# Memory read in the projections' PSUM banks, value sums in one run behind the scores, and a later start of the early modulation rows

## The chip, the cores and the metric

One core of a Trainium2 chip runs the whole program. Its engines are called PE (TensorE, matrix products), PEld (PE's weight loads), DVE (VectorE), ACT (ScalarE), POOL (GpSimd) and SP (SyncE, which issues the DMA transfers). Each engine works through its own instructions in program order. The metric is the device time of one execution in microseconds (us); lower is better.

## The reference

The program is one transformer block over 2048 tokens of 1024 channels, in fp32. Cut to what matters:

```
mod = (silu(c) @ w_mod).reshape(1, 6, 1, 1024)      # sa, ca, ga, sb, cb, gb
h = layernorm(x) * (1 + ca) + sa
x = x + ga * A(h)                                   # attention with a memory
h = layernorm(x) * (1 + cb) + sb
x = x + gb * B(h)                                   # MLP across the tokens
# A: 32 heads of 32 channels, 4 segments s of 512 tokens
q, k, v = h @ wq, h @ wk, h @ wv
for s in range(4):
    a_dot = softmax(q_s k_s^T / sqrt(32) + causal mask) @ v_s
    a_mem = phi(q_s) @ M / (phi(q_s) @ z + 1e-6)    # phi(t) = t + 1 if t > 0 else exp(t)
    o_s   = g * a_mem + (1 - g) * a_dot             # g = sigmoid(beta), per head
    M, z  = M + phi(k_s)^T v_s, z + sum(phi(k_s))
A = o @ wo
# B: W2 gelu(W1 layernorm(h)^T + b1) + b2 along the token axis, 3584 hidden rows
```

## The kernel before

**Stages.** The first 110 us load the modulation, normalize the first segment and transpose it. Then comes the attention, until about 950 us: 32 units of work, each one group of four heads (128 channels) in one segment. The first pass (units 0 to 15) takes segments 0 and 1 of the eight groups in turn, the second pass (units 16 to 31) segments 2 and 3. So odd units, and all units from 16 on, have a segment above 0 and read the memory. After the attention come the product with `wo`, the second normalization, and the token MLP (products named `mx`).

**A unit.** `project(t, piece)` has four pieces. Pieces 0 and 1 make keys and values of half the tokens each: 48 products of 256 columns into a PSUM bank `nps`. Piece 2 transposes the keys (bank `kps`), makes the queries (24 products of 512 columns, bank `qps`), splits both into a high and a low part (`sg`; ACT copies, DVE subtracts) and forms `pq` = phi(q) (two ACT steps on `rq`, then DVE) and `pk` = phi(k). Piece 3 splits the values for the sums (`vp`) and calls `memory(t)`. All these banks have the tag `pj`, of which there are two that are used in turn. A bank is used again when the engines that read its last content are done.

**The memory.** `memory(t)` reads the memory in two halves: PE multiplies `pq` by `MZ` into a bank (tile `rd`), DVE adds 1e-6 to the denominators and inverts them (tile `rdd`) and multiplies (tile `am`, line 454). The sum that updates the memory goes to a tile `up`. Before the change, `rd`, `up`, the transposed row maxima (`nmps`) and the transposed outputs (`ops`) all use the tag `ms`, which is one single bank.

**A head.** Steps are counted in heads, n = 4 t + h, 128 in all. Step n calls `scores` for head n, `maxima` for head n + 3, `values` for head n - 2 and a piece of `project` for head n + 8. `maxima` makes the scores once to find each row's maximum (tiles `sx`, `sy`, `sz` in two banks `s1`; DVE reduces each, line 480, which an order names ISA, a second row reading the maximum out). `scores` makes them again transposed (tiles `a0` of 512 columns, `a1` of 384, `a2` of 128 + 256, in two banks `s2`), ACT takes the exponentials into `p32`, POOL cuts the triangle, ACT copies to fp16 (`ph`, the high part) and POOL subtracts for the low part, which lies in the same tile as `p32`. `values` makes the weighted sums on PE: 10 products of 97 columns with the high part and 10 of 65 with the low part, into the one bank `pv`; DVE then inverts, reduces and scales.

**What sets the order.** The code above is not written in issue order. A scheduler places the instructions of each engine by its own estimate of when operands and banks come free, keeping to data and bank dependencies; `tc.issue_after(x)` and `behind(n, engines)` add the rule that what is inside stands after the marked instruction x. `marks[n, "A"]`, `"G"`, `"V"` hold such instructions of head n for ACT, POOL and DVE. Banks of one tag go round in the order in which the code asks for them: `nps` of both halves, `kps`, `qps`, and again `nps`.

**Extra work between heads.** `plan` and `later` put other steps at a head n: splitting the first pass's weights, normalizing the tokens of later segments (`token_tile`), the columns of the modulation (`mod_fetch` loads 128 rows of `w_mod`, `mod_late` reduces them on DVE, line 573), and the scaling of `wo`. All their loads share three buffers with the tag `raw`.

Of the kernel before, what the change touches and what calls it, by code (L numbers as in the profile page):

```python
# [18 lines left out]
P = 128  # L19
# [8 lines left out]
NV = 97  # L28
# [3 lines left out]
VL = 2  # L32
ML0 = 36
# [8 lines left out]
def attention_and_mlp(ctx, tc, x, wq, wkv, wo, beta, w1, b1, w2, b2, c, wm_a, wm_b, out):  # L42
# [19 lines left out]
    a = par.__enter__()  # L62
# [9 lines left out]
    def bank(tag, bufs, name):  # L72
        return psum.tile([P, 512], F32, tag=tag, bufs=bufs, name=name)
# [367 lines left out]
    def memory(t):  # L441
        pr, g, seg = its[t]
        d = st[t]
        d["am"] = am = b.tile([P, 4, 128], F32, tag="am", bufs=3, name=f"am{t}")
        if seg:
            for half in range(2):
                ps = bank("ms", 1, f"rd{t}_{half}")[:, 0:264].rearrange("p (a n) -> p a n", a=2)
                for aa in range(2):
                    i = 2 * half + aa
                    T.matmul(ps[:, aa], d["pq"][:, 128 * i:128 * i + 128], MZ[:, g], start=True, stop=True)  # L450
# [3 lines left out]
                V.tensor_tensor(am[:, 2 * half:2 * half + 2].rearrange("p a (h e) -> p a h e", h=4),  # L454
                                ps[:, :, 0:128].rearrange("p a (h e) -> p a h e", h=4),
                                rd.unsqueeze(3).to_broadcast([P, 2, 4, 32]), op=ALU.mult)
        if seg < 3:
            ps = bank("ms", 1, f"up{t}")
            for i in range(4):
                T.matmul(ps[:, 0:132], d["pk"][:, i], d["v32"][:, i], start=(i == 0), stop=(i == 3))  # L460
# [46 lines left out]
    def scores(t, h):  # L507
# [10 lines left out]
        T.matmul(b1_[:, 0:384], k[:, 128:256], q[:, 128:512], start=True, stop=True)  # L518
        A.activation(p32[:, 512:896], b1_[:, 0:384], AF.Exp, scale=SCALE, bias=shift)
        b2_ = bank("s2", 2, f"a2_{t}_{h}")  # L520
        T.matmul(b2_[:, 0:128], k[:, 384:512], q[:, 384:512], start=True, stop=True)
        T.matmul(b2_[:, 128:384], k[:, 256:384], q[:, 256:512], start=True, stop=True)  # L522
        A.activation(p32[:, 896:1280], b2_[:, 0:384], AF.Exp, scale=SCALE, bias=shift)  # L523
        for base, step in ((0, 512), (896, 128)):
            w = bass.AP(tensor=p32.tensor, offset=p32.offset + base, ap=[p32.ap[0], [step, 2], [1, 128]])
# [6 lines left out]
    def values(t, h):  # L532
# [7 lines left out]
        for part, w in ((0, NV), (1, 65)):  # L540
            for i in range(4):
                for j in range(i + 1):
                    o = col[j](i)
                    T.matmul(pv[:, i, 0:w], ph[part][:, o:o + 128], d["vp"][:, j, h, 0:w], start=(n == 0),  # L544
                             stop=(n == 19), skip_group_check=True)
                    n += 1
        V.reciprocal(pv[:, :, 0], pv[:, :, 0])
        red = r_.tile([P, 4, 32], F32, tag="red", bufs=2, name=f"red{t}_{h}")
        V.tensor_reduce(red, pv[:, :, 1:97].rearrange("p a (c e) -> p a e c", c=3), axis=AX.X, op=ALU.add)
# [108 lines left out]
    def later(n, fetch, m, f, engines):  # L658

        got = []  # L660
        plan(n, lambda: got.append(fetch()))
        plan(m, lambda: f(got[0]), engines)
# [13 lines left out]
                  n + n1, lambda r, g=g, kind=kind, part=part: split_part(g, kind, part, r), "A")  # L676
        plan(n + 4, lambda g=g: keep_w(g))
    for j in range(32):
        n = ML0 + 2 * j + (8 if j >= 8 else 0)
        later(n, lambda j=j: mod_fetch(j), n + (2 if j < 8 else 1), lambda r, j=j: mod_late(j, r), "V")  # L680
    plan(WO0 - 3, lambda: spread(gaw, 0))
    for i in range(8):
        n = WO0 + WOS * i
# [2 lines left out]
    for n in range(-LEADS, 4 * NI + VL):  # L686
        at(scores, n)
        at(maxima, n + LEADS)
        at(values, n - VL)
        m = n + LEADP  # L690
        if 0 <= m + 4 < 4 * NI:
            t = (m + 4) // 4
# [448 lines left out]
```

## Time and profile before

| | |
|---|---|
| median of 3 runs | 2231.71 us (2225.53 to 2231.82) |
| the profiled execution | 2226.6 us |
| its span, first to last instruction | 2224.9 us |
| PE busy | 2190.3 us |
| DVE busy | 1666.7 us |
| ACT busy | 1135.7 us |
| POOL busy | 725.8 us |
| TensorE clock granted, mean | 0.997 |

How to read the rows that follow: a row of a group of instructions has the source line, the engine, the operation, output<-input, the shape and the number of instructions, then after the bar the busy time in us and the mean length of one in ns, then how long the engine was idle before them and who ended that. PE's products overlap: the length of one product includes its way through the array, so the time that a product takes from the next is the distance of starts and not its length. A row of the timeline has the start in us, the length in us, engine, line and operation, and `xN` for N merged instructions. A row of stretches has the stretch, its length, the busy time of each engine with the count of its instructions, and the granted clock (1.00 is full).

### The profile page before, as it was taken

The page shows a single profiled execution, that of the slowest core. Times are in us where ns is not written, and L with a number is a line of the kernel's source. Part 1 is how long each engine was busy: PE and PEld are TensorE (multiplying, and loading weights), DVE is VectorE, ACT ScalarE, POOL GpSimd, SP SyncE. Part 2 cuts the span into 40 slices and gives each one's busy share as a digit, 9 for nine tenths or more (in the row PEclk, how much of TensorE's full clock was granted, in tenths as well). Part 3 has the DMA queues.
Part 4 walks back from the last instruction along what each step waited for, and adds up shares of the span by engine and source line. Part 5 has one row for each costly group of instructions (what it writes and reads, how often), then busy time and mean ns, then how long its engine had stood idle before and what let it go on. Part 6 is the DMA issues. An engine that isn't in the chain of part 4 may idle for free.

```text
span 2224.9 us, 38052 instructions
## 1 busy us (share of the span) xinstructions
PE 2190.3 (98%) x13786; PEld 1881.0 (85%) x13786; DVE 1666.7 (75%) x3762; ACT 1135.7 (51%) x2050; POOL 725.8 (33%) x831
## 2 busy tenths in 40 slices
PE   8999999999999999999999999999999999999999
PEld 5988898888999999888888888888888888888887
DVE  7676777756777777664858766888888886969687
ACT  5486776756666666654636533533334242424232
POOL 2175766646767776663002200033330000000000
PEclk9999999999999999999999999999999999999999
DMA  7666666686556666664754687655556542414134
GB/s 287 192 187 191 175 181 193 189 279 216 170 180 205 188 183 211 193 219 143 231 194 186 226 304 275 243 223 220 204 202 219 206 148 64 145 57 147 57 123 151
DMA packets 175183, 423.03 MB, mean 190 GB/s; under 512 B 17524, under 2 KB 71828, under 8 KB 166036
## 3 DMA queue, kind: packets, MB, share of 16 engines
q1 hardware_dynamic: 174996, 420.61, 57.5%
q8 instruction: 109, 1.79, 0.3%
q14 instruction: 78, 0.64, 0.1%
HBM read 244.62 MB, written 125.06 MB: 166 GB/s over the span
## 4 chain that ended last, share of the span: by engine, by line
PE 87%; DVE 5%; DMA 3%; ACT 2%; POOL 1%; issue 1%; SPq 0%; DVEq 0%; ACTq 0%
PE mx L921 48%; PE nps L192 11%; PE po L791 8%; PE qps L200 7%; PE pv L544 3%; PE a L515 1%; PE sz L478 1%; PE sx L478 1%; DMA sk<-nt 1%; PE up L460 1%; PE a L518 1%; POOL p L530 1%; PE a L522 1%; PE sy L478 1%; PE rd L450 1%
## 5 line engine op out<-in xcount | busy, mean ns | idle before, releaser
L921 PE MATMUL mx<-bU,sp 128*128 128x512 f32 x2352 | 534.3, 389 | 0.9 <-DVE ac L928 0.9
L921 PEld LDWEIGHTS mx<-bU,sp 128*128 128x128 f32 x2352 | 441.3, 188 | 93.4 <-issue 1.3
L119 ACT CAST sp<-wr 128x384 fp32r<-128x384 f32 (+2 forms) x408 | 218.1, 547 | 431.8 <-PE mx L921 349.1
L192 PE MATMUL nps<-wv,h 128*128 128x256 f32 x3072 | 431.2, 283 | 1.6 <-DVE h L122 0.7
L921 PE MATMUL mx<-bA,sp 128*128 128x512 f32 x1764 | 430.5, 389 | 0.0
L530 POOL TENSOR_TENSOR p<-p,ph 128x640 f16<-128x640 f32 x256 | 380.2, 1485 | 138.5 <-ACT ph L528 134.5
L192 PEld LDWEIGHTS nps<-wv,h 128*128 128x128 f32 x3072 | 400.3, 189 | 9.4 <-DVE h L122 2.0
L921 PEld LDWEIGHTS mx<-bA,sp 128*128 128x128 f32 x1764 | 331.2, 188 | 68.7
L122 DVE TENSOR_TENSOR sp<-wr,sp 128x384 fp32r<-128x384 f32 (+2 forms) x408 | 259.8, 648 | 24.7 <-ACT sp L119 24.4
L928 DVE TENSOR_TENSOR ac<-mx,ac 128x512 f32<-128x512 f32 x280 | 189.9, 687 | 85.2 <-PE mx L921 84.1
L200 PE MATMUL qps<-h,wq 128*128 128x512 f32 x768 | 197.9, 400 | 0.0
L528 ACT CAST ph<-p 128x1280 f16<-128x1280 f32 x128 | 161.4, 1261 | 59.7 <-POOL p L526 59.6
L791 PE MATMUL po<-wo,ots 128*128 128x512 f32 x768 | 180.9, 391 | 0.0
L791 PEld LDWEIGHTS po<-wo,ots 128*128 128x128 f32 x768 | 142.7, 188 | 28.7
L200 PEld LDWEIGHTS qps<-h,wq 128*128 128x128 f32 x768 | 141.6, 190 | 27.7
L921 PE MATMUL mx<-bB,sp 128*128 128x512 f32 x588 | 164.0, 389 | 0.0
L526 POOL TENSOR_SCALAR_AFFINE_SELECT p<-p 128x256 f32<-128x256 f32 x256 | 134.1, 529 | 81.8 <-ACT p L523 53.9
L921 PEld LDWEIGHTS mx<-bB,sp 128*128 128x128 f32 x588 | 110.4, 188 | 22.9
L480 DVE CUSTOM_DVE_ANT_0 sz<-sz,mask 128x512 f32<-128x512 f32 x128 | 89.1, 696 | 52.0 <-PE sz L478 49.5
L480 DVE CUSTOM_DVE_ANT_0 sx<-sx,mask 128x128 f32<-128x128 f32 (+1 forms) x256 | 93.7, 366 | 44.1 <-PE sx L478 37.9
L928 DVE TENSOR_TENSOR cc<-mx,cc 128x512 f32<-128x512 f32 x140 | 94.9, 684 | 37.6 <-PE mx L921 37.4
L516 ACT ACTIVATE p<-a,shift 128x512 f32<-128x512 f32 x128 | 88.4, 691 | 41.2 <-PE a L515 40.4
(209 smaller groups left out, 3244.7 us busy)
## 6 DMA issues: line engine op xcount, KB each, us to landing
sk<-sg SPq DMA_DIRECT2D x384, 128.0 KB
wr<-in_w_dram SPq DMA_DIRECT2D x28, 1024.0 KB
wr<-in_w_dram SPq DMA_DIRECT2D x32, 768.0 KB
bstu<-ucd SPq DMA_DIRECT2D x28, 768.0 KB
wsp<-wv SPq DMA_DIRECT2D x32, 512.0 KB
rawm<-in_wm_b_dram SPq DMA_DIRECT2D x32, 512.0 KB
wv<-wsp SPq DMA_DIRECT2D x32, 512.0 KB
pcd<-cc SPq DMA_DIRECT2D x14, 1024.0 KB
```

What stands on the lines that cost most here:

```text
L119: last_hi[0] = A.copy(hi, src)
L122: return lo_eng.tensor_tensor(lo, src, hi.bitcast(F32), op=ALU.subtract)
L192: T.matmul(ps[:, aa], h[:, j, 128 * tt:128 * tt + 128], wt[:, i, o:o + 256], start=(n == 0), stop=(n >= 6 * NK - 2), skip_group_check=True)
L200: T.matmul(ps, wt[:, i, o:o + 128], h[:, j], start=(k + n == 0), stop=(3 * k + n == 3 * NK - 1))
L480: marks[4 * t + h - LEADS, "V"] = V.tensor_tensor_reduce(o, o, mask[:, 384 - 128 * i:], 1.0, -3.0e38, op0=ALU.add, op1=ALU.max, accum_out= ...
L516: A.activation(p32[:, 0:512], b0, AF.Exp, scale=SCALE, bias=shift)
L526: G.affine_select(w, w, pattern=[[0, 2], [1, 128]], compare_op=ALU.is_ge, fill=0.0, base=0, channel_multiplier=-1)
L528: marks[n, "A"] = A.copy(hi, p32)
L530: marks[n, "G"] = G.tensor_tensor(lo[:, c], p32[:, c], hi[:, c], op=ALU.subtract)
L791: T.matmul(ps, os_[:, i, P * ct:P * ct + P], wop[ct, nh][:, j], start=(n == 0), stop=(n == 3 * NK - 1))
L921: T.matmul(ps, ops[q][:, i, P * k:P * k + P], b[:, j], start=(m == 0 and first), stop=(m == 3 * nk - 1), skip_group_check=True)
L928: V.tensor_tensor(d, ps, d, op=ALU.add)
```

## The change

The change has four parts.

1. The memory's read `rd` takes its two banks from the tag `pj` and no longer from `ms`. So the banks of `pj` now go round as `nps`, `nps`, `kps`, `qps`, `rd`, `rd`, and the next unit's first `nps` uses the bank of the first half of `rd`, its second the bank of the second half.
2. The score products of `a2` are exchanged: 256 columns first, then 128, and the last one is kept as a mark for PE.
3. `values` of head n - 2 stands behind that mark of head n, and its two passes are exchanged and reversed: first the low part (65 columns), then the high part (97 columns), each from the last token tile to the first.
4. The first eight modulation columns (`mod_late` 0 to 7) are fetched at heads 49 to 56 and reduced one head later. Before, they were fetched at every second head from 36 to 50 and reduced two heads later.

```
@@ -444,7 +444,7 @@
         d["am"] = am = b.tile([P, 4, 128], F32, tag="am", bufs=3, name=f"am{t}")
         if seg:
             for half in range(2):
-                ps = bank("ms", 1, f"rd{t}_{half}")[:, 0:264].rearrange("p (a n) -> p a n", a=2)
+                ps = bank("pj", 2, f"rd{t}_{half}")[:, 0:264].rearrange("p (a n) -> p a n", a=2)
                 for aa in range(2):
                     i = 2 * half + aa
                     T.matmul(ps[:, aa], d["pq"][:, 128 * i:128 * i + 128], MZ[:, g], start=True, stop=True)
@@ -518,8 +518,9 @@
         T.matmul(b1_[:, 0:384], k[:, 128:256], q[:, 128:512], start=True, stop=True)
         A.activation(p32[:, 512:896], b1_[:, 0:384], AF.Exp, scale=SCALE, bias=shift)
         b2_ = bank("s2", 2, f"a2_{t}_{h}")
-        T.matmul(b2_[:, 0:128], k[:, 384:512], q[:, 384:512], start=True, stop=True)
-        T.matmul(b2_[:, 128:384], k[:, 256:384], q[:, 256:512], start=True, stop=True)
+        for lo_, hi_, kt in ((128, 384, 2), (0, 128, 3)):
+            marks[n, "P"] = T.matmul(b2_[:, lo_:hi_], k[:, 128 * kt:128 * kt + 128], q[:, 128 * kt:], start=True,
+                                     stop=True)
         A.activation(p32[:, 896:1280], b2_[:, 0:384], AF.Exp, scale=SCALE, bias=shift)
         for base, step in ((0, 512), (896, 128)):
             w = bass.AP(tensor=p32.tensor, offset=p32.offset + base, ap=[p32.ap[0], [step, 2], [1, 128]])
@@ -537,13 +538,12 @@
         col = {0: lambda i: 128 * i, 1: lambda i: 512 + 128 * (i - 1), 2: lambda i: 1024 + 128 * (i - 2),
                3: lambda i: 896}
         n = 0
-        for part, w in ((0, NV), (1, 65)):
-            for i in range(4):
-                for j in range(i + 1):
-                    o = col[j](i)
-                    T.matmul(pv[:, i, 0:w], ph[part][:, o:o + 128], d["vp"][:, j, h, 0:w], start=(n == 0),
-                             stop=(n == 19), skip_group_check=True)
-                    n += 1
+        for part, w in ((1, 65), (0, NV)):
+            for i, j in [(i, j) for i in range(4) for j in range(i + 1)][::-1]:
+                o = col[j](i)
+                T.matmul(pv[:, i, 0:w], ph[part][:, o:o + 128], d["vp"][:, j, h, 0:w], start=(n == 0),
+                         stop=(n == 19), skip_group_check=True)
+                n += 1
         V.reciprocal(pv[:, :, 0], pv[:, :, 0])
         red = r_.tile([P, 4, 32], F32, tag="red", bufs=2, name=f"red{t}_{h}")
         V.tensor_reduce(red, pv[:, :, 1:97].rearrange("p a (c e) -> p a e c", c=3), axis=AX.X, op=ALU.add)
@@ -676,8 +676,8 @@
                   n + n1, lambda r, g=g, kind=kind, part=part: split_part(g, kind, part, r), "A")
         plan(n + 4, lambda g=g: keep_w(g))
     for j in range(32):
-        n = ML0 + 2 * j + (8 if j >= 8 else 0)
-        later(n, lambda j=j: mod_fetch(j), n + (2 if j < 8 else 1), lambda r, j=j: mod_late(j, r), "V")
+        n = 49 + j if j < 8 else ML0 + 2 * j + 8
+        later(n, lambda j=j: mod_fetch(j), n + 1, lambda r, j=j: mod_late(j, r), "V")
     plan(WO0 - 3, lambda: spread(gaw, 0))
     for i in range(8):
         n = WO0 + WOS * i
@@ -686,7 +686,8 @@
     for n in range(-LEADS, 4 * NI + VL):
         at(scores, n)
         at(maxima, n + LEADS)
-        at(values, n - VL)
+        with behind(n, "P"):
+            at(values, n - VL)
         m = n + LEADP
         if 0 <= m + 4 < 4 * NI:
             t = (m + 4) // 4
```

The order that results, as rows of the built programs. In the names, the number behind the letters is the unit (and then head) that it belongs to.

**PE between the last query product of unit 22 and the first key and value product of unit 23.** Before:

```order
L200 MATMUL qps22_10407<-h2_7_7309,wq1_3_0_1_9720 128x512
L515 MATMUL a0_20_3_10457<-sk0_3_500 128x512
L478 MATMUL sy_21_2_10478<-sk1_2_503 128x384
L478 MATMUL sz_21_2_10481<-sk1_2_503 128x512
L192 MATMUL nps23_0_10625<-wv1_3_0_0_9710,h3_0_7399 128x256 x6
L192 MATMUL nps23_0_10625<-wv1_3_0_0_9710,h3_1_7401 128x256 x6
L192 MATMUL nps23_0_10625<-wv1_3_0_1_9712,h3_2_7521 128x256 x3
L486 MATMUL nmps21_1_10363<-ident_90,mx21_0_10237 8x128
```

After, where the next product of unit 23 stands 148 rows behind the last query product of unit 22:

```order
L478 MATMUL sx_22_0_10705<-sk0_0_497 128x256
L515 MATMUL a0_21_1_10689<-sk1_1_502 128x512
L478 MATMUL sy_22_0_10710<-sk0_0_497 128x384
L450 MATMUL rd22_0_10521<-MZ_127,pq22_10437 128x132 x2
L450 MATMUL rd22_1_10528<-MZ_127,pq22_10437 128x132 x2
L478 MATMUL sz_22_0_10713<-sk0_0_497 128x512
L518 MATMUL a1_21_1_10692<-sk1_1_502 128x384
L522 MATMUL a2_21_1_10695<-sk1_1_502 128x256
L522 MATMUL a2_21_1_10695<-sk1_1_502 128x128
L478 MATMUL sx_22_1_10819<-sk0_1_498 128x128
L478 MATMUL sx_22_1_10819<-sk0_1_498 128x256
L460 MATMUL up22_10535<-v32_22_10165,pk22_10442 128x132 x4
```

and then, behind the 20 sums of head 3 of unit 20:

```order
L544 MATMUL pv20_3_10716<-vp20_9615,ph20_3_10456 128x97
L478 MATMUL sy_22_1_10824<-sk0_1_498 128x384
L486 MATMUL nmps21_3_10574<-ident_90,mx21_2_10472 8x128
L478 MATMUL sz_22_1_10827<-sk0_1_498 128x512
L192 MATMUL nps23_0_10625<-wv1_3_0_0_9710,h3_0_7387 128x256 x6
L192 MATMUL nps23_0_10625<-wv1_3_0_0_9710,h3_1_7389 128x256 x6
```

Before, the keys of unit 23 follow the queries of unit 22 after three score products, and the memory's read of unit 22 comes some sixty rows later among them. Now both reads (`rd22_0`, `rd22_1`) come first, and what stands between the two units' projections is scores, row maxima and sums of about three heads each.

**DVE, the memory's read of unit 22.** Before:

```order
L452 TENSOR_SCALAR rdd22_0_10524<-rd22_0_10521 128x8
L438 TENSOR_TENSOR vp22_10513<-r1_22_10514,vp22_10513 128x16x32
L453 RECIPROCAL rdd22_0_10524<-rdd22_0_10524 128x8
L480 ISA sx_22_0_10705,mx22_0_10704<-sx_22_0_10705,mask_93 128x128
L480 ISA mx22_0_10704 128x1
L454 TENSOR_TENSOR am22_10520<-rd22_0_10521,rdd22_0_10524 128x256
L480 ISA sx_22_0_10705,mx22_0_10704<-sx_22_0_10705,mask_93 128x256
L480 ISA mx22_0_10704 128x1
L452 TENSOR_SCALAR rdd22_1_10531<-rd22_1_10528 128x8
L547 RECIPROCAL pv20_2_10584<-pv20_2_10584 128x4
L453 RECIPROCAL rdd22_1_10531<-rdd22_1_10531 128x8
```

After:

```order
L573 SCALAR_TENSOR_TENSOR rawm20_10676,mcol_529<-rawm20_10676,scb_76 128x1024
L453 RECIPROCAL rdd22_0_10524<-rdd22_0_10524 128x8
L438 TENSOR_TENSOR vp22_10513<-r1_22_10514,vp22_10513 128x16x32
L480 ISA sx_22_1_10819,mx22_0_10704<-sx_22_1_10819,mask_93 128x128
L480 ISA mx22_0_10704 128x1
L453 RECIPROCAL rdd22_1_10531<-rdd22_1_10531 128x8
L465 TENSOR_TENSOR tm22_10540<-up22_10535,bdg_128 128x132
L547 RECIPROCAL pv20_3_10716<-pv20_3_10716 128x4
L480 ISA sy_22_1_10824,mx22_0_10704<-sy_22_1_10824,mask_93 128x384
L480 ISA mx22_0_10704 128x1
L454 TENSOR_TENSOR am22_10520<-rd22_0_10521,rdd22_0_10524 128x256
```

The rows `L452`, `L453` and `L454` with `rd22_0` are the read of the first bank. Before, three other rows lie between the first and the last of them. Now a column of the modulation, the low part of the values (`vp22`), two score reductions of a later head and the memory's update stand ahead of line 454.

**PE around the sums.** Before (head 2's last score products, between sums of head 0 of unit 20):

```order
L544 MATMUL pv20_0_10373<-vp20_9615,ph20_0_10101 128x97
L544 LDWEIGHTS p32_20_0_10100
L544 MATMUL pv20_0_10373<-vp20_9615,p32_20_0_10100 128x65
L521 MATMUL a2_20_2_10343<-sk0_2_499 128x128
L522 MATMUL a2_20_2_10343<-sk0_2_499 128x256
L544 LDWEIGHTS p32_20_0_10100
```

After (head 0 of unit 21, then the sums of head 2 of unit 20, which now stand together):

```order
L478 MATMUL sz_21_3_10571<-sk1_3_504 128x512
L522 MATMUL a2_21_0_10554<-sk1_0_501 128x256
L522 MATMUL a2_21_0_10554<-sk1_0_501 128x128
L544 LDWEIGHTS p32_20_2_10335
L544 MATMUL pv20_2_10584<-vp20_9615,p32_20_2_10335 128x65
```

The 128-column product is now the last one ahead of the sums. In the whole program the sums stood in 289 pieces before and stand in 139 now; 226 pieces were followed by a score or projection product and 112 are now. In 72 places the 128-column product is directly followed by sums.

More of the change, by code (lines that the diff above doesn't have):

```diff
@@ L446, in memory @@
             for half in range(2):
[L447 removed]
+                ps = bank("pj", 2, f"rd{t}_{half}")[:, 0:264].rearrange("p (a n) -> p a n", a=2)
                 for aa in range(2):
@@ L688, in attention_and_mlp @@
         at(maxima, n + LEADS)
-        at(values, n - VL)
+        with behind(n, "P"):
+            at(values, n - VL)
         m = n + LEADP
```

22 lines of the change are left out of this document (11 added, 11 removed).

## The prediction

> **What bounds the kernel now.** I read the page's busy times first, then the waits of PE, then the stretches, and last the timeline around one unit of the attention.
>
> ```profile
> span 2224.9 us, 38052 instructions
> PE 2190.3 (98%) x13786; PEld 1881.0 (85%) x13786; DVE 1666.7 (75%) x3762; ACT 1135.7 (51%) x2050; POOL 725.8 (33%) x831
> ```
>
> PE is busy almost without a gap, so the time is the length of its list plus its waits. The profiled execution took 2226.6 us, 1.7 over the span, and 5.1 below the median of the runs (2231.71). Changes below some 7 us (0.3%) can't be told from none.
>
> ```profile
> PE up L460 <- DVE am L454: 3.8, 3, 3.5
> 600.00:700.00 100.00, 99.31 (x884) 90.95 (x884) 69.91 (x222) 62.78 (x110) 68.62 (x84) 1.00 0.66 207
> 1200.00:1400.00 200.00, 200.00 (x884) 165.66 (x883) 139.67 (x225) 86.01 (x161) 17.54 (x12) 1.00 0.70 258
> ```
>
> The first row is PE's wait for the memory's read in the single `ms` bank, 3.5 us of it in one place. The second is a stretch of the attention: DVE (third pair) works 70 of 100 us there, beside PE. The third is the MLP, where 884 products of 512 columns take 200 us: 0.226 us each, 0.44 ns a column. The MLP's code isn't changed, so the whole question is the attention.
>
> There PE is full because 96 key and value products per unit are at hand whenever scores or sums must wait. One unit (22), its last query product, the first key and value product of the next unit, and DVE's last step of the first memory read:
>
> ```profile
> 697.58 0.33 PE L522 MATMUL a<-sk 98*128 98x256 f32 x1
> 697.75 0.45 PE L544 MATMUL pv<-vp,p 128*128 128x65 bf16 x9
> 698.04 0.51 PE L200 MATMUL qps<-h,wq 128*128 128x512 f32 x1
> 698.38 0.41 PE L515 MATMUL a<-sk 98*128 98x512 f32 x1
> ...
> 699.03 1.42 PE L192 MATMUL nps<-wv,h 128*128 128x256 f32 x11
> ...
> 709.68 0.41 DVE L454 TENSOR_TENSOR am<-rd,rdd 128x256 f32<-128x256 f32 x1
> 710.02 0.42 DVE L480 CUSTOM_DVE_ANT_0 sx<-sx,mask 128x256 f32<-128x256 f32 x1
> ```
>
> The next unit's products begin 1.0 us after the last query product starts; the read is done 11.5 us after that product ends (710.09 - 698.55). DVE's next row starts 0.07 us before the read's last step ends: its rows overlap.
>
> **Part 1, the memory's read in the projections' banks.** The banks of tag `pj` go round in turn, so the first `nps` of unit t + 1 now has to wait until line 454 has emptied the first `rd` of unit t. That holds for 23 pairs of units (1, 3, ... 15 and 16 to 30). Until then PE has only scores, row maxima, sums and the memory's products. What that costs is the hold (queries' end to line 454) less PE's work in it.
>
> The hold, from the trace of before: unit 15, the last of the first pass, then 16, 19 (the shortest) and 30 of the second, as pairs of the last run of query products and line 454:
>
> ```profile
> 491.59 1.86 PE L200 MATMUL qps<-h,wq 128*128 128x512 f32 x7
> 511.31 0.42 DVE L454 TENSOR_TENSOR am<-rd,rdd 128x256 f32<-128x256 f32 x1
> 521.71 3.60 PE L200 MATMUL qps<-h,wq 128*128 128x512 f32 x15
> 535.34 0.42 DVE L454 TENSOR_TENSOR am<-rd,rdd 128x256 f32<-128x256 f32 x1
> 611.92 0.95 PE L200 MATMUL qps<-h,wq 128*128 128x512 f32 x3
> 621.24 0.42 DVE L454 TENSOR_TENSOR am<-rd,rdd 128x256 f32<-128x256 f32 x1
> 921.83 1.78 PE L200 MATMUL qps<-h,wq 128*128 128x512 f32 x7
> 935.34 0.41 DVE L454 TENSOR_TENSOR am<-rd,rdd 128x256 f32<-128x256 f32 x1
> ```
>
> That is 18.3, 10.4, 8.8 and 12.1 us. Read like this, the 15 units of the second pass have 8.8 to 13.8, mean 11.3; the 8 of the first 8.7 (unit 1) to 22.9, mean 16.8, because DVE also splits that pass's weights there.
>
> PE's work in the hold, from the order of unit 22 after: twelve score outputs of 384 columns and five of 512, 7168 columns at 0.44 ns, 3.2 us. Three times 20 sums, 0.75 us each:
>
> ```profile
> 709.03 0.61 PE L544 MATMUL pv<-vp,ph 128*128 128x97 bf16 x10
> 673.16 0.47 PE L544 MATMUL pv<-vp,p 128*128 128x65 bf16 x10
> 706.45 0.61 PE L450 MATMUL rd<-MZ,pq 128*128 128x132 f32 x4
> ```
>
> The distance of starts is (0.61 - 0.21) / 9 = 45 ns and (0.47 - 0.20) / 9 = 30 ns, and for `rd` 0.11 us a pass; `rd` and `up` are 16 passes, 1.8 us. With `nmps` that is 7.4 us, and 8.0 with what short products and ends of sums leave uncovered (six times 0.06 and three times 0.1, priced under parts 2 and 3). So PE stands 11.3 - 8.0 = 3.3 us in each of 15 units and 16.8 - 8.0 = 8.8 in each of 8: 50 + 70 = 120 us.
>
> A second way, by the changed order of DVE for unit 22. Between the queries' split and the first line 454 stand 39 rows, 27 of them these:
>
> ```profile
> L480 DVE CUSTOM_DVE_ANT_0 sz<-sz,mask 128x512 f32<-128x512 f32 x128 | 89.1, 696 | 52.0 <-PE sz L478 49.5 <-PE pv L544 2.0
> L480 DVE CUSTOM_DVE_ANT_0 sy<-sy,mask 128x384 f32<-128x384 f32 x128 | 73.7, 576 | 13.7 <-PE sy L478 13.2
> L480 DVE DVE_READ_ACCUMULATOR2_ANT mx<- 128x1 f32 x512 | 71.7, 140 | 0.0
> L549 DVE TENSOR_REDUCE red<-pv 128x128 f32<-128x384 f32 x128 | 70.7, 552 | 5.7 <-DVE pv L547 0.5
> L480 DVE CUSTOM_DVE_ANT_0 sx<-sx,mask 128x256 f32<-128x256 f32 x128 | 55.7, 435 | 1.1
> L573 DVE SCALAR_TENSOR_TENSOR rawm<-rawm,scb 128x1024 f32<-128x1024 f32 x32 | 49.5, 1548 | 8.4 <-DMA rawm<-in_wm_b_dram 8.2
> L480 DVE CUSTOM_DVE_ANT_0 sx<-sx,mask 128x128 f32<-128x128 f32 x128 | 38.0, 297 | 43.0 <-PE sx L478 37.9 <-PE nmps L486 4.7
> L438 DVE TENSOR_TENSOR vp<-r,vp 128x512 bf16<-128x512 f32 x32 | 31.2, 976 | 3.1 <-ACT vp L437 2.8
> L436 DVE TENSOR_TENSOR r<-v,vp 128x512 f32<-128x512 f32 x32 | 25.1, 785 | 3.4 <-ACT vp L435 3.3
> L426 DVE SCALAR_TENSOR_TENSOR pk<-k,rk 128x512 f32<-128x512 f32 x24 | 20.8, 868 | 0.0
> L419 DVE SCALAR_TENSOR_TENSOR pq<-qps,rq 128x512 f32<-128x512 f32 x24 | 16.5, 686 | 5.1 <-ACT rq L417 5.1
> ```
>
> In the order of the rows, 2, 3, 10, 2, 2, 1, 3, 1, 1, 1 and 1 of them are 12.2 us as single lengths. The 12 others are short (inversions, `rdd`, `red`, `sg`, `tm`, `am`); at an estimated 0.28 each, between the short rows above (140 and 435 ns), they are 3.4. Rows overlap by some 0.08, 38 times, 3.0 us. So DVE needs 12.6 us and begins one copy of ACT and a signal later, estimated 0.9 from such copies of 0.6: 13.5, less 8.0 is 5.5, and 23 times that 127. I take 124, between the two ways. Bounds: the shortest hold in every unit, 23 x 0.8 = 18; and no overlap of DVE's rows, 23 x 8.5 = 196.
>
> Queued behind the waiting `nps` on PE are all later scores; DVE's work goes on, so it is ahead once the projection runs, and can't be used then: PE is the bound again. What the change takes away is the `ms` wait quoted above, 3.8 us, and with it this:
>
> ```profile
> 128.00:131.00 3.00, 1.85 (x8) 1.23 (x8) 2.69 (x12) 3.00 (x7) 2.31 (x5) 1.00 1.06 267
> 133.00:136.40 3.40, 3.40 (x23) 3.19 (x23) 2.76 (x3) 3.40 (x8) 3.13 (x3) 0.50 1.00 260
> 452.00:454.00 2.00, 0.00 (x0) 0.00 (x0) 2.00 (x3) 1.72 (x4) 1.51 (x2) 0.96 1.02 383
> 456.00:460.00 4.00, 4.00 (x32) 3.73 (x31) 3.08 (x8) 2.57 (x5) 1.09 (x5) 0.50 1.00 386
> ```
>
> After the long wait at 452 the clock was granted at 0.50 for some 10 us (to 464), 5 us lost. Together -9. But the same rows price the new stalls: after 128 to 131, where PE was busy 1.85 of 3 us with waits of about 1 us, the clock fell to 0.50 for 3.4 us too, 1.7 us lost. If half of the 23 stalls do that, +20 (bounds 0 and 23 x 5 = 115). The Trainium skill (page "TensorE: Matmul & The Clock Gate", section "Part 1: The HAM clock gate") says that the gate halves the clock after an idle window of about 3.4 us; by that rule alone single waits of 1 to 3 us between scores would not trip it, the term would be 0 and the time 20 us lower. The row at 133 speaks against so mild a reading, so I keep the half.
>
> **Parts 2 and 3, the order of scores and sums.** After a piece of sums the next big product takes longer: the query product of 698.04 is followed after 0.34 us instead of 0.226. 114 fewer such returns at 0.1 are -11. The 256-column product behind the 128-column one takes 0.17 (697.58 to 697.75) against 0.113 for 256 columns; with the short one last and sums behind it, whose weight loads are short, 72 x 0.057 = -4. Together -15 (bounds 0 and -25). Later sums delay DVE's and POOL's steps on them, which nothing but the next sums needs: 0.
>
> **Part 4, the modulation.** 8 x 1.55 us of DVE move from units 11 to 14 to units 14 to 16, and eight loads of 512 KB move past the key loads in SP's queue; the DMA engines are busy 0.66 in the row of 600 to 700, which covers them. What the holds gain early they lose late: 0 (bounds -5 and +5).
>
> **Sum.** 2226.6 + 124 - 9 + 20 - 15 = 2346.6; with the 5.1 by which the median lies higher, 2352.
>
> **Rivals.**
> - The other side: DVE empties the first `rd` within PE's 8.0 us in nearly all units. Then only -9 and -15 stay: 2208. It decides where the hold is below 9 us; units 1 and 19 come near it (8.7, 8.8), the other 21 don't. 0.05.
> - Stall and gain cancel, as the chain through PE were shorter than I count (1 us a unit): 2232. 0.03.
> - The clock falls in every stall, at times for 10 us: +60 to +115 instead of +20, 2392 to 2447. For it the row at 133, against it the waits of about 1 us elsewhere in the span, whose mean clock is still 0.997. 0.15.
> - POOL becomes the bound, since the low part, its last step, is now needed first:
>
> ```profile
> L530 POOL TENSOR_TENSOR p<-p,ph 128x640 f16<-128x640 f32 x256 | 380.2, 1485 | 138.5 <-ACT ph L528 134.5
> L526 POOL TENSOR_SCALAR_AFFINE_SELECT p<-p 128x256 f32<-128x256 f32 x256 | 134.1, 529 | 81.8 <-ACT p L523 53.9 <-ACT p L519 27.1
> ```
>
> Two of each are 4.0 us a head, three heads 12.1 in a hold of 13.5. If one subtraction is missing each time, 23 x 1.5 = +35: 2387. 0.10.
> - My case, DVE's list sets the hold, keeps 0.67; its own range is 2290 to 2400.
>
> The range reaches from 3.5 us of stall a unit (80 - 24 = +56, 2288) to 7.5 us with the clock falling once in each (172 + 39 - 24 = +187, 2419). Slower: 0.67 + 0.15 + 0.10; same 0.03; faster 0.05.
>
> **What would show it.** PE's waits must have new rows for DVE: score products for line 480, and `nps` for line 454, together over 80 us, none of that size behind 1100 us. The attention should end near 1070 instead of 950 and the MLP keep its 0.226 us a product. Pieces of sums should lie behind the 128-column product without a gap. I am wrong if `nps` follows the queries without PE waits, or if the waits name POOL or DMA.

## The result, and the profile after

The kernel with the change took 2367.93 us (median of 5 runs, 2365.16 to 2369.83), the kernel before on the same chip 2231.71 us (5 runs). The ratio is 1.0617, with a 95% interval of 1.0601 to 1.0634: 136 us slower. The first part of the page of after:

```profile
span 2368.1 us, 38129 instructions
PE 2260.3 (95%) x13786; PEld 1933.5 (82%) x13786; DVE 1669.7 (71%) x3762; ACT 1133.8 (48%) x2050; POOL 729.4 (31%) x831
```

The span grew by 143.2 us. PE's busy time grew by 70.0 and its idle time (span less busy) by 73.2, from 34.6 to 107.8. The busy times of DVE, ACT and POOL change by less than 4 us each. So PE stands more, and its products take longer.

Where that happened, by the stretches of after (busy time of PE, its weight loads, DVE, ACT and POOL, then the granted clock):

```profile
600.00:700.00 100.00, 90.52 (x747) 80.38 (x748) 63.23 (x199) 53.22 (x93) 62.24 (x71) 0.93 0.52 152
800.00:900.00 100.00, 85.89 (x678) 76.71 (x678) 63.06 (x192) 53.26 (x92) 56.73 (x69) 0.88 0.53 154
1200.00:1400.00 200.00, 200.00 (x884) 165.62 (x883) 151.05 (x333) 112.01 (x219) 19.91 (x13) 1.00 0.60 209
```

Between 600 and 700 us PE issues 747 products where it issued 884 before, and the clock is 0.93 instead of 1.00. The MLP has kept its 884 products in 200 us. All of the loss lies in the attention, as the first and last products with `wo` show (the rows are of before, then of after; the columns are the least, median and longest length in ns, and the first and last start):

```profile
L791 PE MATMUL po<-wo,ots x768: 387/389/480, 955.9 to 1153.1; 128*128 128x512 f32 x192
```

```profile
L792 PE MATMUL po<-wo,ots x768: 387/389/478, 1106.4 to 1296.3; 128*128 128x512 f32 x192
```

The last one starts 143.2 us later, which is the whole growth of the span.

PE's waits in after (total, times, longest):

```profile
PE sz L478 <- DVE mx L480: 23.5, 33, 1.6
PE sx L478 <- DMA sk<-sg: 10.2, 10, 3.5
PE sy L478 <- DVE mx L480: 9.9, 14, 2.3
PE a L515 <- DMA sk<-nt: 7.7, 4, 3.7
...
PE sx L478 <- DVE mx L480: 4.4, 6, 2.3
...
PE nps L192 <- DVE am L454: 0.8, 1, 0.8
```

The largest new rows are score products that wait until DVE has reduced the bank ahead of them (line 480). Line 454 itself is named for 0.8 us only, since other products, score products mostly, stand in front of `nps` in PE's order and wait first. Unit 22, the one shown before the change, from the timeline of after (the bracket is the idle time just before, with who ended it):

```profile
773.24 1.31 PE L200 MATMUL qps<-h,wq 128*128 128x512 f32 x5
...
776.93 0.51 PE L478 MATMUL sz<-sk 96*128 96x512 f32 x1 [0.32 <-DVE mx L480]
...
779.49 0.47 PE L478 MATMUL sx<-sk 96*128 96x128 f32 x2 [0.53 <-DMA sk<-sg]
...
780.20 1.06 PE L450 MATMUL rd<-MZ,pq 128*128 128x132 f32 x8
782.46 0.50 PE L478 MATMUL sz<-sk 96*128 96x512 f32 x1 [1.20 <-DVE mx L480]
...
784.11 2.11 PE L460 MATMUL up<-v,pk 128*128 128x132 f32 x8 [0.35 <-DVE pk L426]
...
788.60 0.49 PE L478 MATMUL sz<-sk 96*128 96x512 f32 x1 [0.61 <-DVE mx L480]
788.97 1.74 PE L192 MATMUL nps<-wv,h 128*128 128x256 f32 x13
```

and DVE's step that sets the bank free:

```profile
788.40 0.42 DVE L454 TENSOR_TENSOR am<-rd,rdd 128x256 f32<-128x256 f32 x1
```

The queries end at 774.55, line 454 ends at 788.82, and the next unit's products start at 788.97. Before the change they started 1.0 us after the last query product did. Over the 23 pairs of units, the mean from the start of the last query product is now 14.6 us to the end of the first line 454, and 15.3 us to the next `nps` (10.8 to 19.7); in each pair `nps` starts after line 454 ends. In 10 of the 23 pairs it starts 0.15 us after that end, as in unit 22 (788.82 to 788.97), so that the bank was the last thing it waited for; in the other 13 it starts 0.3 to 1.7 us after it, behind other products of PE's order.

The hold of unit 22 and the stretch behind it, with the same columns as the stretches above:

```profile
774.45:789.00 14.55, 11.24 (x102) 9.24 (x100) 12.71 (x41) 10.21 (x17) 9.13 (x15) 0.88 0.71 181
789.00:800.00 11.00, 11.00 (x97) 11.00 (x97) 3.86 (x10) 3.37 (x7) 7.84 (x7) 1.00 0.65 217
```

DVE is the busiest engine in the hold, 12.71 of 14.55 us. Over all 23 holds DVE is busy 90% of the time, PE 76%, ACT 72% and POOL 69%.

To see what fills these holds I compared each start distance on PE with the median distance that the same product, between the same neighbours, has in the trace of before. What exceeds it inside a stretch of half clock, up to a doubling, is put down to the clock; the rest is standing. The median itself is the work. A hold runs here from the start of the last query product to the next unit's first `nps`; before the change there is hardly one.

| kernel | mean hold, us | work in it | standing in 23 holds | half clock in 23 holds | standing in the rest of the attention | half clock there |
|---|---|---|---|---|---|---|
| before | 1.6 | 1.4 | 5 | 0 | 27 | 5 |
| after | 15.3 | 7.8 | 123 | 50 | 11 | 14 |
| e2, part 1 alone | 13.9 | 7.0 | 105 | 53 | 8 | 5 |
| e1, parts 2 to 4 | 1.8 | 1.4 | 8 | 0 | 46 | 10 |
| e4, read asked for later | 1.3 | 1.2 | 3 | 0 | 76 | 29 |
| e5, ACT empties the bank | 13.3 | 6.4 | 104 | 53 | 12 | 7 |
| e10, short maxima | 11.1 | 6.7 | 79 | 22 | 5 | 0 |

From before to after that is +118 of standing and +50 of half clock in the holds, +9 of half clock and -16 of standing elsewhere, -12 of work (the medians of all products add up to 2149.9 us instead of 2162.2), and -6 that the working leaves over: +143. (The medians of the runs differ by 136 us; the profiled execution of before was 5.1 us below its median, that of after 1.9 above.)

These sizes are estimates, since they depend on which neighbours are compared. With other choices (the product behind alone, or the one ahead as well) the holds of after have 114 to 123 us of standing and 50 to 53 of half clock; outside the holds standing falls by 10 to 31 us, and the work of all products changes by +4 to -20. So the columns for the holds are firm, and the division of the gain outside them into standing and work is not.

### The profile page after: what moved, and what is told of

It is laid out like the page before. It is cut to its first block, busy times and chain, and to the rows that moved or that the text cites. A ratio compares the mean times of both kernels' runs of the same rounds, so it can differ in the third digit from the quotient of the medians.

```text
span 2368.1 us, 38129 instructions
## 1 busy us (share of the span) xinstructions
PE 2260.3 (95%) x13786; PEld 1933.5 (82%) x13786; DVE 1669.7 (71%) x3762; ACT 1133.8 (48%) x2050; POOL 729.4 (31%) x831
## 4 chain that ended last, share of the span: by engine, by line
PE 83%; DVE 9%; DMA 3%; ACT 2%; issue 2%; POOL 1%; SPq 0%; DVEq 0%; ACTq 0%
PE mx L922 44%; PE nps L192 14%; PE qps L200 7%; PE po L792 7%; PE pv L544 3%; PE sz L478 1%; PE sx L478 1%; PE a L515 1%; PE up L460 1%; DVE rawm L573 1%; DMA sk<-sg 1%; DVE sx L480 1%; PE rd L450 1%; DVE sy L480 1%; DVE sz L480 1%
## 5 line engine op out<-in xcount | busy, mean ns | idle before, releaser
L531 POOL TENSOR_TENSOR p<-p,ph 128x640 f16<-128x640 f32 x256 | 385.3, 1508 | 85.8 <-ACT ph L529 81.6
L192 PE MATMUL nps<-wv,h 128*128 128x256 f32 x3072 | 401.2, 286 | 2.4 <-DVE am L454 0.8
L192 PEld LDWEIGHTS nps<-wv,h 128*128 128x128 f32 x3072 | 385.6, 194 | 8.9 <-DVE h L122 2.0
L200 PE MATMUL qps<-h,wq 128*128 128x512 f32 x768 | 193.1, 397 | 0.0
L547 DVE RECIPROCAL pv<-pv 128x4 f32<-128x4 f32 x128 | 24.1, 188 | 136.2 <-PE pv L544 135.9
```

The costliest lines, as they stand in the source:

```text
L192: T.matmul(ps[:, aa], h[:, j, 128 * tt:128 * tt + 128], wt[:, i, o:o + 256], start=(n == 0), stop=(n >= 6 * NK - 2), skip_group_check=True)
L200: T.matmul(ps, wt[:, i, o:o + 128], h[:, j], start=(k + n == 0), stop=(3 * k + n == 3 * NK - 1))
L531: marks[n, "G"] = G.tensor_tensor(lo[:, c], p32[:, c], hi[:, c], op=ALU.subtract)
```

## The experiments

Times are medians; each ratio is to the kernel before on the same chip, with its 95% interval.

**e1: the change without part 1.** `rd` goes back into the single bank `ms`.

```diff
-                ps = bank("pj", 2, f"rd{t}_{half}")[:, 0:264].rearrange("p (a n) -> p a n", a=2)
+                ps = bank("ms", 1, f"rd{t}_{half}")[:, 0:264].rearrange("p (a n) -> p a n", a=2)
```

> The changed kernel with part 1 undone: the memory's read is back in the single ms bank, parts 2, 3 and 4 stay. If the rotation of the projections' banks makes the loss, nearly all of it goes: 2210 to 2235 us, the next unit's keys start about 1 us after the queries again, and the half-clock stretches fall from 28 to a few. If the sums in one run behind the scores (part 3) starve PE, most of the loss stays: above 2300 us.

**e2: part 1 alone**, the same line changed the other way in the kernel before.

> The kernel before with part 1 alone: only the two banks of the memory's read change their tag. If the rotation makes the loss: 2340 to 2390 us (the packing gain of parts 2 and 3 is missing, the finer mix of scores and sums may give some of it back), and the first nps of a unit starts within 0.5 us after line 454 of the unit before. If part 3 makes the loss: 2215 to 2250 us.

e1 took 2235.07 us, 1.0044 (1.0031 to 1.0057). e2 took 2353.55 us, 1.0577 (1.0561 to 1.0594). The two ratios multiply to 1.0623, against 1.0617 for the whole change. So the loss is part 1's, and parts 2 to 4 cost a little where 15 us of gain were forecast. e1 came out at the upper edge of what was expected, with 26.3 us of half clock in 6 stretches. e2 lies in its range, but `nps` starts within 0.5 us of line 454 in only 13 of its 23 pairs, and 0.76 us after it on average.

**e3: parts 2 and 3 alone**, the kernel before with the score products exchanged, and the sums reversed and placed behind them.

> Parts 2 and 3 alone, the memory's read in ms and the modulation as before. By my price (fewer pieces of sums, the 128-column product last) 15 us less than before: 2210 to 2225 us. If the order of scores and sums makes new waits of the same size: 2225 to 2240 us. If it makes the loss: above 2300 us.

2230.95 us, 1.0016 (1.0006 to 1.0027). This is the second of the expected ranges, with no gain. The two parts were then taken singly.

**e7: part 2 alone**, the 256-column product first:

```diff
-        T.matmul(b2_[:, 0:128], k[:, 384:512], q[:, 384:512], start=True, stop=True)
-        T.matmul(b2_[:, 128:384], k[:, 256:384], q[:, 256:512], start=True, stop=True)
+        for lo_, hi_, kt in ((128, 384, 2), (0, 128, 3)):
+            marks[n, "P"] = T.matmul(b2_[:, lo_:hi_], k[:, 128 * kt:128 * kt + 128], q[:, 128 * kt:], start=True,
+                                     stop=True)
```

> The kernel before with part 2 alone: the 256-column product of a2 ahead of the 128-column one. If the uncovered weight load behind a 128-column product is worth 0.057 us a head where sums follow, and sums follow in a third of the heads: 2 us less, within the noise, 2220 to 2232 us. A loss over 7 us would mean that the order, which the scheduler changes with it, costs more than the product.

**e8: part 3 alone**, with the mark on the last product of the old order:

```diff
+        for lo_, hi_, kt in ((0, 128, 3), (128, 384, 2)):
+            marks[n, "P"] = T.matmul(...)
...
-        at(values, n - VL)
+        with behind(n, "P"):
+            at(values, n - VL)
```

> The kernel before with part 3 alone: the sums in one run behind the last score product (here the 256-column one), low part first. By my price for fewer returns from sums (-11 us) 2210 to 2222 us; if the sums in one run take from PE the filler between scores, the gain is eaten by new waits: 2225 to 2245 us.

e7 took 2235.87 us, 1.0035 (1.0021 to 1.0048), some 8 us more than before, where 2 less were expected; by what was written ahead, a loss over 7 us means that the changed order costs more than the product gains. e8 took 2234.12 us, 1.0031 (1.0019 to 1.0043), in the range named for a gain that new waits eat up. Each is slightly slower. By the working of the table the gain in PE's own distances is there: the medians of all products add up to 2151.0 us in e3, 2150.8 in e1 and 2149.4 in e8, 11 to 13 less than the 2162.2 of before. In e7 it is only 1.9. But PE stands more than before: 54.2 us over the whole attention in e1, 49.0 in e3, 45.9 in e8 and 43.1 in e7, instead of 31.1. With other neighbours the gain is 5 to 25 us in e1 and e3 and the added standing 5 to 26, so the sizes are loose. The pages need no medians and point the same way: PE's busy time falls by 4.7 us in e1 and 7.8 in e3, and its idle time grows by 13.1 and 10.1. The waits of e1 and e3:

```profile
PE sz L478 <- DVE mx L480: 7.5, 8, 2.9
...
PE a L515 <- DMA sk<-nt: 5.7, 7, 1.3
PE sx L478 <- DMA sk<-sg: 5.3, 5, 1.9
```

```profile
PE a L515 <- DMA sk<-nt: 6.1, 4, 1.8
PE sx L478 <- DMA sk<-sg: 4.8, 5, 1.2
PE sz L478 <- DVE mx L480: 3.7, 4, 2.0
```

Score products now wait for the row maxima, and for the keys' and the maxima's transfers. Of the rows of after, about half of the waits for these transfers (11.0 of 20.5 us in all rows of that kind) are there in e1 too, where part 1 is undone.

**e11: part 4 alone**, the early modulation columns at heads 49 to 56.

> The kernel before with part 4 alone: the first eight modulation columns from head 49 on. By my price 0: 2225 to 2235 us. The DVE work that it moves away from heads 36 to 50 could free the long wait of PE at 451 us (4 us and 5 us of half clock): then 2215 to 2225 us.

2229.31 us, 0.9993 (0.9982 to 1.0005): no change. The one long wait of before at 452 us isn't in this trace, which has 4.0 us of half clock in place of 15.2. By the start distances the half clock costs 4 us less there, and standing in other places and the work take that back: nothing is left.

**e4: the read asked for after the next unit's keys and values.** The order in which the code asks for banks of `pj` becomes `nps`, `nps`, `rd`, `rd`, `kps`, `qps`, with `rd` of the unit before. So `nps` no longer depends on the read, and `kps` and `qps` do. The memory's update `MZ += tm` is moved behind the read.

```diff
+            if half and t and its[t - 1][2]:
+                read(t - 1)
...
-    def memory(t):
+    def read(t):
...
-                G.tensor_tensor(MZ[:, g], MZ[:, g], tm, op=ALU.add)
```

> The changed kernel with the read still in the pj banks, but asked for (and issued) after the next unit's keys and values, and the memory's update added behind it. So the same banks and the same work, and the next unit's nps no longer waits for it. If the hold of line 454 on the next unit's projection makes the loss: 2205 to 2245 us. If using pj for the read costs by itself (its banks then wait for queries or transposes): above 2300 us.

2271.42 us, 1.0199 (1.0183 to 1.0215). This lies outside what was expected: by the ratios the change of order takes back 4.2 of the 6.2% of loss, some 93 us, but not all. By the table there is no hold any more. The order moved a smaller one to another place: from the start of the last `nps` product to that of the first query product it is now 6.05 us on average (units 3 to 31), against 3.92 in e1 and 3.36 before. One unit, from the timeline of e4:

```profile
744.89 1.88 PE L192 MATMUL nps<-wv,h 128*128 128x256 f32 x15
746.61 0.61 PE L452 MATMUL rd<-MZ,pq 128*128 128x132 f32 x4
...
748.45 0.68 PE L452 MATMUL rd<-MZ,pq 128*128 128x132 f32 x4
...
750.12 0.60 PE L407 MATMUL kps<-ident,k 128*128 128x128 f32 x4
...
752.59 4.62 PE L200 MATMUL qps<-h,wq 128*128 128x512 f32 x19
```

After the products of `nps` come both reads, and `kps` and `qps` must wait for them: in each of the 23 units behind a unit that reads the memory, `kps` starts after DVE's last step of the first read has ended, in 7 of them within 0.2 us. The use of the `pj` banks is the same as in after, and two thirds of the loss are gone; so it is the place in the turn that costs, more than the sharing of two banks.

**e5: ACT copies the read out of the bank**, and DVE works on the copies. This tells whether DVE's step on the bank, or the whole list of work, holds `nps`.

```diff
-                V.tensor_scalar_add(rd, ps[:, :, 128:132], 1e-6)
+                ah = am[:, 2 * half:2 * half + 2].rearrange("p a (h e) -> p a h e", h=4)
+                A.copy(rd, ps[:, :, 128:132])
+                A.copy(am[:, 2 * half:2 * half + 2], ps[:, :, 0:128])
+                V.tensor_scalar_add(rd, rd, 1e-6)
...
+                V.tensor_tensor(ah, ah, rd.unsqueeze(3).to_broadcast([P, 2, 4, 32]), op=ALU.mult)
```

> The changed kernel, but ACT copies the memory's products out of their pj bank (two copies a half, numerators and denominators), and DVE then works on the copies. If the time at which line 454 empties the first bank sets the loss, the bank comes free some 3 to 4 us earlier and most of 23 times that comes back: 2280 to 2310 us. If the time up to pq and the read's products on PE is what holds, or PE starves on the scores' own banks anyway, little comes back: 2340 to 2370 us.

2350.08 us, 1.0552 (1.0532 to 1.0571): only 0.65% of before, some 14 us, better than after, as expected for the case that PE waits for other things anyway. The bank is free after 11.0 us on average instead of 14.6, but `nps` starts after 13.3, and never sooner than 1.1 us after the bank is free. The run's waits:

```profile
PE sy L479 <- DVE mx L481: 19.7, 21, 2.2
PE sz L479 <- DVE mx L481: 19.5, 20, 3.0
```

The score products that stand ahead of `nps` in PE's order wait for DVE's maxima all the same. By the table the hold is 2.0 us shorter, but 1.3 of that (7.77 to 6.44) is work, which then has to be done later; standing in the holds falls by 0.8 us a unit, 19 us in all; the spans differ by 20.1.

**e6: work for the hold.** Twelve products of 512 columns without use are put ahead of the first `rd` half, in its bank, 24 times: 288 products, 65 us at full clock.

```diff
+                full = bank("pj", 2, f"rd{t}_{half}")
+                for _ in range(FILL[half]):
+                    T.matmul(full, W[pr, g]["q", 0][:, 0, 0:128], hpages[seg, 0][:, 0], start=True, stop=True)
```

> The changed kernel with 12 more products of 512 columns ahead of the first half of the memory's read, into that bank, which the read then overwrites (24 units, 65 us of PE work at 0.226 us each; they compute nothing that is used). The stalls keep PE at the full clock. If the half clock behind the stalls is a large part of the loss (some 60 us by the stretched products of the trace), the half-clock stretches fall from 28 to under 10 and the time falls in spite of the added work or stays: 2310 to 2370 us. If the clock costs little and only the waits count, the fill lies partly in the waits and partly adds: 2370 to 2430 us.

2372.69 us, 1.0651 (1.0635 to 1.0667), against 1.0617 for after. The added products were meant to keep PE busy, and with it at the full clock, in the stalls. Their 65 us are almost free (some 8 us of difference by the ratios), so they do lie in time in which PE stood or would have. The half clock falls from 169.4 us in 28 stretches to 112.7 in 19, not to under 10, and the time doesn't fall with it. By the start distances (the product behind alone) the work grows by 60 us, while standing falls by 34 and what the half clock costs by 23, which leaves the 3 us by which the spans differ. As to how much of the loss is the clock's, the run is inconclusive: filling the hold moves PE's other work in it as well.

**e9 and e10: a shorter list of DVE**, in before (e9) and in after (e10). The row maxima look at the first 16 columns of each score tile only, which leaves the rest of the maxima out; the scores are scaled by 0.01 more so that the exponentials stay small.

```diff
-                    o, o, mask[:, 384 - 128 * i:], 1.0, -3.0e38, op0=ALU.add, op1=ALU.max,
+                    o[:, 0:16], o[:, 0:16], mask[:, 384 - 128 * i:][:, 0:16], 1.0, -3.0e38, op0=ALU.add, op1=ALU.max,
```

> The kernel before with shorter work on DVE: the row maxima are taken over the first 16 columns of each score tile alone (line 480: some 0.15 us instead of 0.30 to 0.70, about 1.4 us less a head), and the scores' factor is 0.01 of the reference's so that the exponentials stay finite. It leaves the rest of each row out of the maximum. PE bounds the kernel before, so little changes: 2215 to 2235 us.

> The same two edits on the changed kernel, with the same part of the maxima left out. If DVE's list sets the stretch between a unit's queries and the next unit's keys, some 4 us of DVE's 13 to 15 go from it, and the difference to the same edit on the kernel before falls from 140 to between 50 and 100 us: 2275 to 2325 us. If the stretch is set by ACT, POOL or transfers, the difference stays at 120 to 140 us: above 2340 us.

e9 took 2237.33 us, 1.0032 (1.0019 to 1.0044), 2 us above what was expected and no faster: DVE is not what limits the kernel before. e10 took 2283.06 us, 1.0236 (1.0209 to 1.0263). With the shorter maxima the change costs 46 us instead of 136. The page of e10:

```profile
span 2279.9 us, 38060 instructions
PE 2204.7 (97%) x13786; PEld 1895.7 (83%) x13786; DVE 1526.6 (67%) x3762; ACT 1134.0 (50%) x2050; POOL 735.9 (32%) x831
```

DVE has 143 us less to do than in after. The hold falls from 15.3 to 11.1 us, its standing from 123 to 79 and all half clock from 64 to 22; together with 6 us less of standing elsewhere that is 92 us less, where the time fell by 85. DVE's 143 us are 4.5 a unit, and the hold is 4.2 shorter: DVE's list in the hold sets its length. DVE remains the busiest engine in the holds of e10 too, at 86%.

No kernel here beats the one before.

## Why the prediction was right, and where it was not

**The direction and the mechanism: right.** 2368 us lie in the range of 2288 to 2419, 16 above the 2352 of the forecast. Part 1 costs it (e2), by the new dependence of `nps` on line 454 (e4 takes it away and most of the loss with it), with DVE's list as the length of the hold (e10). Line 454 alone isn't the hold: when ACT empties the bank earlier, the score products ahead of `nps` still wait for DVE (e5).

That the time is only 16 us off is partly luck. In the profiled executions a growth of 120 us was forecast (124 - 9 + 20 - 15), and it is 143. The clock cost 44 us more than forecast and parts 2 and 3 brought 3 less; against that, standing outside the holds fell by 12 more, the stall was 6 smaller, and 6 are left over. Another 7 us of the difference lie between the profiled executions and the medians.

**The stall, 124 us: right in size.** Standing in the 23 holds is 123 us, 118 more than before. PE's work in a hold was put at 8.0 us and is 7.8. The way by DVE's list put the time from the end of the queries to line 454 at 13.5 us; unit 22 shows 14.3 (774.55 to 788.82), and that is the mean of the 23 too. The other way, by the trace of before, had the right mean (13.2) with the wrong shares: it put 16.8 us in the first pass's units and 11.3 in the second's, and after has 15.2 and 13.8. The hold is some 1 us longer than forecast, and the half clock takes 2.2 us of it, so standing comes out as forecast by two errors that cancel in part.

**The clock, +20 less 5 for the half clock taken away: the step that failed.** It was mis-sized. The working let half of the 23 stalls halve the clock for 3.4 us. In fact there are 27 stretches of half clock in the attention, 167 us, 6.2 us each on average. They cost 64 us of product time by the table, 59 more than before, where 15 were forecast. Two neighbouring windows in unit 22 show one case:

```profile
780.75:784.16 3.41, 1.87 (x12) 1.33 (x10) 3.41 (x10) 2.28 (x5) 3.08 (x4) 1.00 0.89 193
784.16:787.57 3.41, 3.41 (x29) 3.34 (x29) 3.13 (x11) 1.23 (x2) 1.90 (x4) 0.50 0.97 316
```

No single wait in the first is longer than 1.20 us, but PE was busy in only 1.87 of 3.41 us, and the next 3.41 us run at 0.50. The rule of the Trainium skill that the prediction weighed (page "TensorE: Matmul & The Clock Gate", "Part 1: The HAM clock gate": half clock after an idle window of about 3.4 us) would have made this term 0; these rows go against so narrow a reading. In the same Part 1 of the Trainium skill's page the section "A second HAM failure mode: psum-queue depth-cycling" tells of a kernel whose short idle times between groups were enough to make the clock swing; the two windows above, with no wait over 1.20 us, agree with it. The rival "the clock falls in every stall" (2392 to 2447, chance 0.15) had the size of this term right at its low end: +60 less 5, where 59 were measured. Its time was still 24 us too high, because the terms that came out lower than forecast, named above, then have nothing against them.

**The removed wait in `ms`, -4: too small.** Standing outside the holds fell by 16 us by the table (10 to 31 with other neighbours), not by 3.8. Probably this is because DVE, ACT and the transfers get ahead while PE is held, so that nobody is late during the next projection's run. DVE's own waits show the other side of it, first before, then after:

```profile
DVE pv L547 <- PE pv L544: 53.5, 46, 5.2
```

```profile
DVE pv L547 <- PE pv L544: 135.9, 50, 12.8
```

DVE runs out of work while PE works through the projection, up to 12.8 us at a time, as the prediction said.

**Parts 2 and 3, -15: half right.** Their gain in PE's distances is 12 us in after by the table's working, with the reserve made under the table. The mechanism is seen: a weight load of the score products takes 190 ns on average in the trace of before and one of the sums 98, and a 128-column product with sums right behind it is no longer followed by a delay.

```profile
774.56 0.34 PE L522 MATMUL a<-sk 98*128 98x256 f32 x2
774.74 0.49 PE L544 MATMUL pv<-vp,p 128*128 128x65 bf16 x10
```

The sums start 0.18 us after the first of the two products; 384 columns at 0.44 ns are 0.17. In all 72 places where sums follow the 128-column product of after, the median distance is 0.063 us; before, the 256-column product behind the 128-column one took 0.17. What failed is the price of 0 for later sums ("which nothing but the next sums needs"): alone (e1, e3) the new order makes PE stand 18 to 23 us more by the table's working, with the waits shown there, and the gain is gone.

**Part 4, 0: right** (e11).

**What would show it.** The attention ended 150 us later by its first `wo` product and 143 by its last, where 120 were forecast, and the MLP kept its 0.226 us a product. Waits of score products for line 480 and of `nps` for line 454 were to come to over 80 us; the rows name 37.8 and 0.8, half of that. The sum of standing is right, but its labels aren't all DVE's: all listed waits of PE grew from 30.7 to 102.5 us, of which those for DVE by 44.7, those for transfers by 23.2. Waits that name DMA were a sign of being wrong, and this sign is there in part. The transfers `sk<-sg` carry a unit's freshly split keys and queries to its scores; with no projection products left to do, PE has reached them.

**POOL as the bound: refuted.** The one wait of the sums for POOL's steps on the exponentials is (line 527 cuts the triangle)

```profile
PE pv L544 <- POOL p L527: 1.2, 1, 1.2
```

What stays open is how much of the clock's 50 us inside the holds would be standing if the clock didn't fall. e6 was to tell, and doesn't. No run changes only the place that `nps` has in PE's order, with the banks as in after, so how much of the hold is the order's alone isn't shown either.

## What to carry to other kernels

Before a tile is moved to another group of banks, write out the turn of the banks with the new tile in it, and look at which later user waits for which engine's list; here a read whose last step comes some 14 us after the queries stood directly ahead of the products that kept PE full. Freeing the bank earlier (e5) or making one engine faster (e10) gives back a part only; another place in the turn (e4) gives back more. When a stall is priced on PE, price the half clock that follows it by the busy share of the window, and not by the longest single wait.

## What the runs showed of the hardware that was not expected

The stretches of half clock of one trace begin on a fixed grid, to within 0.01 us, and last whole multiples of 3.41 us (3.41, 6.83, 10.24, 13.65), apart from one that the end of the program cuts short. In after I divided 84 to 1108 us into 300 windows on that grid. 26 windows at full clock were followed by one at half clock, and PE was busy in 0.50 to 2.35 of their 3.41 us. Of the windows that were followed by full clock, only three had less than 2.3 us. The two ends, and the lowest one that was followed by full clock:

```profile
1060.64:1064.05 3.41, 0.50 (x1) 0.19 (x1) 3.41 (x10) 2.61 (x4) 2.22 (x4) 1.00 0.92 242
```

```profile
272.16:275.57 3.41, 2.35 (x25) 1.56 (x25) 2.89 (x12) 3.41 (x7) 2.42 (x2) 1.00 0.48 119
```

```profile
135.63:139.04 3.41, 2.08 (x27) 1.48 (x26) 2.81 (x13) 3.41 (x7) 2.74 (x3) 1.00 1.02 397
```

So in this trace the clock fell when PE had been busy for less than some 60 to 70% of such a window. The trace of before has one case above that: 2.64 us busy from 129.56 to 132.98, and half clock behind it. The same count over all thirteen traces gives a wider border: of the windows at full clock, every one with less than 1.6 us busy was followed by half clock, of those with more than 2.65 us a single one (3.00 us, in e10), and between the two both happened.

At half clock the same run of 48 `nps` products takes 7.73 us instead of 5.70, and the ten sums of 97 columns 1.01 instead of 0.61:

```profile
722.94 5.70 PE L192 MATMUL nps<-wv,h 128*128 128x256 f32 x48
752.38 7.73 PE L192 MATMUL nps<-wv,h 128*128 128x256 f32 x48
...
775.06 0.61 PE L544 MATMUL pv<-vp,ph 128*128 128x97 bf16 x10
...
786.58 1.01 PE L544 MATMUL pv<-vp,ph 128*128 128x97 bf16 x10
```

The slower run of 48 is only partly at half clock (until 756.9 us). The page counts PE as busy in such stretches, not as slow: its 95% hide the 64 us.
